# Attention and two feed-forward layers on one core: new fixed costs for VectorE in the scheduler's table, and a new set of priorities

## The chip, the cores and the metric

The kernel runs on 1 core of one Trainium2 chip. TensorE (PE) does the matmuls, VectorE (DVE), ScalarE (ACT) and GpSimd (POOL) the elementwise work, and SyncE (SP) issues every DMA on one hardware queue. The metric is the device time of one execution in microseconds: the median of several runs.

## The reference

Masked attention over 4 batches, 8 heads, 576 positions and head size 64, followed by two feed-forward layers over the 2304 resulting tokens (model size 512, inner size 2048). The weights and alpha come as float64.

```python
scores = scale * np.matmul(q, k.transpose(0, 1, 3, 2))
mask = block_i >= block_j            # blocks of 64 positions
scores = np.where(mask, scores, -1000000000.0)
scores = scores - np.max(scores, axis=-1, keepdims=True)
attn = np.exp(scores)
attn = attn / (np.sum(attn, axis=-1, keepdims=True) + 1e-09)
x = np.matmul(attn, v)               # then heads side by side: [2304, 512]
h = x @ w_in;  x = (np.maximum(h, 0.0) + alpha * np.minimum(h, 0.0)) @ w_out
h = x @ w_in2; x = (h * (1.0 / (1.0 + np.exp(-1.702 * h)))) @ w_out2
```

## The kernel before

**Attention** runs in 20 passes: for batch 0 four head pairs with the first 320 queries and then the same four with the other 256; for batches 1 to 3 one pass per head pair with both groups of queries. Of a pass, PE transposes q and k (tile `tp`, line 345), ACT and DVE split them into a high and a low part (tiles `k`, `ks`, `qs`; lines 120, 123, 388), and PE makes negated scores (tile `sc`, line 441). DVE masks and takes the minimum of each row (lines 455, 456), ACT takes the exponential with its row sum (tile `e`, line 464), DVE the reciprocal of the sums (tile `stat`, lines 473, 474), POOL the fp16 high part of the normalised weights and DVE its fp16 remainder (tile `hl`, lines 486, 494). A DMA transposes `hl` into `pt` (line 498). PE multiplies `pt` with the values (tile `pv`, line 519), and ACT and DVE add the two halves of `pv` into `x` (lines 531, 532). Transposes `tp` and products `pv` share two PSUM buffers (tag `tv`), so that the next `tp` or `pv` but one waits for line 532 of a `pv`.

**The feed-forward layers** use each matmul three times, with high and low parts in fp32r. While attention still runs, PE does half of the first layer's inner features (8 of 16 blocks `f`) for token blocks of 288: line 207 (tile `h`), the gate on ACT and DVE (lines 215, 216), the split on ACT and POOL (tile `gs`), and the second product (tile `x2`, lines 245 to 247). After attention come the other 8 blocks of the first layer and then the second layer, in token blocks of 384 (lines 207, 218, 219, 653, 663, 666). Each weight block of 128 x 512 float64 words is loaded as integers (tile `rw`), and turned into fp32 by ACT and three DVE instructions (lines 150, 153, 155, 156; tiles `wa`, `sq`), then split (`wh`, `wl`). Matmuls of a small constant tile (`warm`, line 584) fill gaps on PE at the start.

**The order of the instructions** is made by the program itself. The functions put pieces of work on a list, each with a place in time plus a value by kind: `at()` adds `0.1 * ORDER[kind] + SHIFT[kind]`. After everything has been recorded, `arrange()` (line 782 on) plays the work through a model: it keeps for each engine a heap of the instructions that are ready, takes the one with the lowest value as soon as the engine is free, adds the duration that `cost()` (line 758 on) gives, and writes the order that results as fixed dependencies. The engines then run their queues strictly in this order. So the table in `cost()` decides when something is ready in the model, and `SHIFT` which of the ready pieces goes first.

```python
    def at(kind, n, fn):
        plan.append((n, ORDER[kind], len(plan), fn, n + 0.1 * ORDER[kind] + SHIFT.get(kind, 0)))
```

The lines that the change touches are the table `SHIFT` (lines 48 to 55) and one line of `cost()` (line 776), for DVE: reads of PSUM with fewer than three operands, instructions under 8 elements, and `tensor_reduce`.

Of the kernel before, what the change touches and what calls it, by code (L numbers as in the profile page):

```python
# [45 lines left out]
    "split x 2": 8, "load w": 9, "load w 2": 9, "load x": 9, "load k": 9.5, "load q": 9.5, "load v": 9.5, "load alpha": 9.6,  # L46
}
SHIFT = {
    "gate": -44.2, "gate 2": -23, "gemm1": 56.7, "gemm1 2": 12.5, "gemm2": 12.8, "half": 58.9, "half out": -42,
    "high": -6.3, "load alpha": 27.7, "load k": 56.1, "load q": -37.1, "load v": -27.1, "load w": -32.6,  # L50
    "load w 2": -53.5, "load x": -33, "narrow": 56.5, "narrow 2": -25.1, "norm": -46.2, "out": -53.7,
    "prep out": 42.4, "prep t": 41.2, "prep v": 41.6, "pv": -10, "pv out": -41.9, "rest": 40.6, "score": 51.7,
    "setup": -24.2, "soft": 19, "split g": -43.8, "split g 2": 4.8, "split w": 7.8, "split w 2": -28.1,
    "split x": 26.4, "split x 2": 57.1, "warm": 56.9,
}
BIG = 1.0e30

# [655 lines left out]
def free_size(ap):  # L713
    n = 1
    for _, c in list(ap.ap)[1:]:
        n *= c
    return n
# [40 lines left out]
def cost(eng, kind, ins, outs):  # L758

    n = max(free_size(a) for a in ins + outs)  # L760
    psum = any(a.tensor.space == PSUM for a in ins)
    if eng == "PE":
        mv, w = ins[:2]
        cols, load = free_size(outs[0]) * (2 if mv.dtype == F32 else 1), free_size(w)
        rows = list(w.ap)[0][1]
        each = 13.3 if mv.dtype == F32R else 2.7
        return cols / 2.4 + each, load / 1.2 + 13.3 if BYTES[w.dtype] == 4 else load / 4.8, cols * rows / 128, mode(w)
    if eng == "Activation":
        return (50 if psum else 93) + n / 1.2 + (187 if len(outs) > 1 else 0),
    full = sum(free_size(a) == n for a in ins)  # L770
    if eng == "Pool":
        return (35 + n / 1.2 if not ins else 244 + n / 1.2 if full < 2 else 148 + 2.1 * n),
    if not ins:
        return (40 if outs[0].tensor.space == PSUM else 7) + n / 1.92,
    if psum and len(ins) < 3 or n < 8 or kind == "InstTensorReduce":
        return 65 + n / 0.96,
    if full < 2:
        return 64 + n / 1.92,
    return (129 if len(ins) > 2 else 68) + n / 0.96,
# [174 lines left out]
```

## Time and profile before

| | |
|---|---|
| median of 3 runs | 1086.78 us (1085.62 to 1089.73) |
| profiled execution | 1087.33 us, its span 1085.5 us |
| PE busy | 1021.4 us (94% of the span), 6454 matmuls |
| DVE busy | 604.3 us (56%), 1029 instructions |
| ACT, POOL busy | 494.7 us (46%), 462.4 us (43%) |
| DMA | 120.28 MB, 111 GB/s |
| mean granted TensorE clock | 0.982 of 2.4 GHz |

The shares are means over stages with different limits. The page's slices cut the span into 40 equal parts of 27.1 us; attention ends near 423 us, and from about 484 us on PE is nearly always busy. In the rows below, "idle before" is the time in which an engine stood still just ahead of an instruction, with the instruction whose end let it go on.

### The profile page before, as it was taken

To read this page: it belongs to the slowest core of one execution; us is meant where nothing else is said; L and a number is where in the kernel's file an instruction comes from. 1 tells how busy PE (TensorE), PEld (TensorE's weight loads), DVE (VectorE), ACT (ScalarE), POOL (GpSimd) and SP (SyncE) were. 2 spreads that over 40 slices of the span, in tenths; PEclk is the share of its full clock that TensorE was granted. 3 is DMA by queue.
4 is the path that set the end of the run, shared out by engine and by line. 5 is a ranking of instruction groups with operands and counts; after the bars stand their busy time and mean duration, and the time that the engine had idled before them with its cause. 6 is when DMAs were issued, how large, how long until landed. Compare 5 with 4: busy or idle time off the path is not lost. (4 is left out here: it accounts for less than half of the span.)

```text
span 1085.5 us, 17180 instructions
## 1 busy us (share of the span) xinstructions
PE 1021.4 (94%) x6454; PEld 934.3 (86%) x6454; DVE 604.3 (56%) x1029; ACT 494.7 (46%) x1164; POOL 462.4 (43%) x494
## 2 busy tenths in 40 slices
PE   7776978999999999999999999999999999999998
PEld 4554867989898899999999999899999999999997
DVE  7888998788888885778883236831111121211110
ACT  5664765666566564565543235433223232322322
POOL 4565864656666574644432233422222222222221
PEclk8888999999999999999999999999999999999999
DMA  7897989788989765544643225401000010000000
GB/s 190 189 209 156 209 188 187 138 176 155 175 154 175 147 124 140 168 141 157 202 144 126 81 65 183 146 8 59 1 30 30 1 59 1 30 30 1 30 1 30
DMA packets 257284, 120.28 MB, mean 111 GB/s; under 512 B 213936, under 2 KB 250800, under 8 KB 257200
## 3 DMA queue, kind: packets, MB, share of 16 engines
q1 hardware_dynamic: 257200, 119.18, 46.1%
q8 instruction: 51, 0.84, 0.3%
q14 instruction: 33, 0.27, 0.1%
HBM read 68.82 MB, written 18.87 MB: 81 GB/s over the span
## 5 line engine op out<-in xcount | busy, mean ns | idle before, releaser
L123 POOL TENSOR_TENSOR gs<-g,gs 128x384 fp32r<-128x384 f32 (+1 forms) x208 | 212.8, 1024 | 452.4 <-ACT gs L120 431.8
L207 PE MATMUL h<-xh,wh 128*128 128x384 f32 (+1 forms) x832 | 272.2, 327 | 6.8 <-ACT xo L251 3.7
L207 PE MATMUL h<-xh,wl 128*128 128x384 f32 (+1 forms) x832 | 270.2, 325 | 0.0
L219 DVE TENSOR_TENSOR g<-g,h 128x384 f32<-128x384 f32 x96 | 53.1, 553 | 291.6 <-ACT g L218 291.6
L653 PE MATMUL acc<-wh,gs 128*128 128x512 f32 x576 | 194.9, 392 | 1.5 <-DVE o L663 1.5
L207 PE MATMUL h<-xl,wh 128*128 128x384 f32 x576 | 193.1, 335 | 0.0
L207 PEld LDWEIGHTS h<-xh,wh 128*128 128x128 f32 x832 | 156.3, 188 | 15.3 <-ACT xo L251 5.2
L207 PEld LDWEIGHTS h<-xh,wl 128*128 128x128 f32 x832 | 156.4, 188 | 0.1
L120 ACT ACTIVATE gs<-g 128x384 fp32r<-128x384 f32 (+1 forms) x208 | 103.3, 498 | 106.7 <-DVE g L219 60.9
L218 ACT ACTIVATE g<-h 128x384 f32<-128x384 f32 x96 | 47.0, 490 | 191.6 <-PE h L207 191.6
L486 POOL TENSOR_SCALAR hl<-e,stat 64x64 f16<-64x64 f32 (+4 forms) x160 | 107.7, 688 | 57.1 <-DVE stat L474 28.0
L653 PEld LDWEIGHTS acc<-wh,gs 128*128 128x128 f32 x576 | 108.1, 188 | 22.4 <-DVE o L663 1.3
L494 DVE SCALAR_TENSOR_TENSOR hl<-e,stat,hl 64x64 f16<-64x64 f32 (+4 forms) x160 | 122.7, 800 | 5.7 <-POOL hl L486 4.7
L653 PE MATMUL acc<-wl,gs 128*128 128x512 f32 x288 | 113.7, 395 | 0.0
L207 PEld LDWEIGHTS h<-xl,wh 128*128 128x128 f32 x576 | 108.1, 188 | 4.1
L519 PE MATMUL pv<-pt,vp 128*128 128x256 f16 (+2 forms) x960 | 88.1, 248 | 14.6 <-DMA pt<-hl 10.5
L464 ACT ACTIVATE e<-sc,stat 64x64 f32<-64x64 f32 (+4 forms) x160 | 82.8, 520 | 34.0 <-DVE hl L494 19.2
L653 PE MATMUL acc<-gs,wh 128*128 128x384 f32 x384 | 98.1, 335 | 0.2 <-DVE o L663 0.2
L216 DVE SCALAR_TENSOR_TENSOR g<-g,nalph,h 128x288 f32<-128x288 f32 (+1 forms) x112 | 61.6, 551 | 58.4 <-ACT g L215 57.4
L519 PEld LDWEIGHTS <-vp 128*128 128x128 bf16 x960 | 64.6, 102 | 27.6 <-DMA pt<-hl 14.9
L123 POOL TENSOR_TENSOR wl<-sq,wh 128x512 fp32r<-128x512 f32 x40 | 59.5, 1488 | 61.7 <-ACT wh L120 61.6
L245 PE MATMUL x<-gs,wh 128*128 128x288 f32 x256 | 75.7, 302 | 2.9 <-ACT wh L120 2.4
(65 smaller groups left out, 1708.4 us busy)
## 6 DMA issues: line engine op xcount, KB each, us to landing
rw<-in_moe_w_in_dram SPq DMA_DIRECT2D x32, 512.0 KB, 4.2
rw<-in_moe_w_out_dram SPq DMA_DIRECT2D x32, 512.0 KB, 3.8
nat_q<-in_q_dram SPq DMA_DIRECT2D x24, 288.0 KB, 4.1
nat_k<-in_k_dram SPq DMA_DIRECT2D x16, 288.0 KB, 3.6
nat_v<-in_v_dram SPq DMA_DIRECT2D x16, 288.0 KB, 4.5
xa<-xo SPq DMA_DIRECT2D x32, 144.0 KB, 2.5
o<-xa SPq DMA_DIRECT2D x24, 192.0 KB, 2.5
xl<-xs SPq DMA_DIRECT2D x6, 768.0 KB, 4.9
```

Of the source, the lines that this page charges most:

```text
L120: act.activation(out=dst, in_=src, func=ACTF.Copy, scale=scale_)
L123: eng.tensor_tensor(out=dst, in0=src, in1=hi.bitcast(F32), op=ALU.subtract)
L207: pe.matmul(ps, st_[:, sl], mv[:, c], start=z == 0, stop=z == 3 * KD - 1)
L216: dve.scalar_tensor_tensor(out=g, in0=g, scalar=nalph[:, f:f + 1], in1=ps, op0=ALU.mult, op1=ALU.add)
L218: act.activation(out=g, in_=ps, func=ACTF.Sigmoid, scale=1.702)
L219: dve.tensor_tensor(out=g, in0=g, in1=ps, op=ALU.mult)
L245: pe.matmul(ps, oh[:, sl], gh, start=f == 0, stop=False)
L464: act.activation(out=eo, in_=v[:, h] if len(heads) > 1 else v, func=ACTF.Exp, scale=-1.0, bias=stat[0:m, 0, a:a + 1], accum_out=stat[0:m, ...
L486: pool.tensor_scalar(out=o, in0=e, scalar1=r, scalar2=1.0, op0=ALU.mult, op1=ALU.mult)
L494: dve.scalar_tensor_tensor(out=hl_part(j, 1, m, nk, h), in0=es[h][0:m, off:off + nk], scalar=stat[0:m, 2, 2 * a + h:2 * a + h + 1], in1=hl ...
L519: pe.matmul(o, l, r, start=z == 0, stop=z == len(ops) - 1)
L653: pe.matmul(ps, a, b_, start=f == f0 and z == 0, stop=f == NF - 1 and z == 2)
```

## The change

One line of the DVE price in `cost()` goes from 65 ns to 155 ns of fixed time for instructions of 8 or more elements, and all 33 values of `SHIFT` are replaced. No instruction is added, removed or changed; the queues hold the same instructions in another order.

```diff
 SHIFT = {
-    "gate": -44.2, "gate 2": -23, "gemm1": 56.7, "gemm1 2": 12.5, "gemm2": 12.8, "half": 58.9, "half out": -42,
...
+    "gate": -35, "gate 2": -14, "gemm1": 42.8, "gemm1 2": 46.1, "gemm2": 47.4, "half": 42.2, "half out": -36.5,
...
     if psum and len(ins) < 3 or n < 8 or kind == "InstTensorReduce":
-        return 65 + n / 0.96,
+        return (65 if n < 8 else 155) + n / 0.96,
```

SP, the first instructions of its queue, before: loads of `q`, `v`, the first weight block, `k` and alpha.

```order
L322 DMA nat_q<-in_q_dram 128x7x64
L325 DMA nat_v<-in_v_dram 128x7x64
L137 DMA rw<-in_moe_w_in_dram 128x4x128
L325 DMA nat_k<-in_k_dram 128x9x64
L574 DMA nalph<-in_moe_alpha_dram 128x16x1
L322 DMA nat_q<-in_q_dram 128x7x64
```

And now:

```order
L325 DMA nat_k<-in_k_dram 128x9x64
L322 DMA nat_q<-in_q_dram 128x7x64
L137 DMA rw<-in_moe_w_in_dram 128x4x128
L325 DMA nat_v<-in_v_dram 128x7x64
L574 DMA nalph<-in_moe_alpha_dram 128x16x1
L322 DMA nat_q<-in_q_dram 128x7x64
```

The load of `k` has gone from the fourth place to the first; the second load of `q` (the same rows, for the other half of the partitions) is still the sixth.

DVE in batch 1, about 189 us into the trace of before: `x` from the product `pv_2124` of one pass, and the six remainders `hl00`, `hl01` of the next pass, before:

```order
L473 TENSOR_SCALAR stat0_100<-stat0_100 128x6
L474 RECIPROCAL stat0_100<-stat0_100 128x6
L532 SCALAR_TENSOR_TENSOR x_1765<-pv_2124,x_1765 64x256
L494 SCALAR_TENSOR_TENSOR hl00_96<-e_2077,stat0_100,hl00_96 64x64
L455 MEMSET sc_2240 64x64
L494 SCALAR_TENSOR_TENSOR hl00_96<-e_2077,stat0_100,hl00_96 128x192
L216 SCALAR_TENSOR_TENSOR g_2222<-g_2222,nalph_78,h_2191 128x288
L494 SCALAR_TENSOR_TENSOR hl00_96<-e_2156,stat0_100,hl00_96 128x320
L494 SCALAR_TENSOR_TENSOR hl01_97<-e_2078,stat0_100,hl01_97 64x64
L216 SCALAR_TENSOR_TENSOR g_2311<-g_2311,nalph_78,h_2253 128x288
L494 SCALAR_TENSOR_TENSOR hl01_97<-e_2078,stat0_100,hl01_97 128x192
```

And now:

```order
L494 SCALAR_TENSOR_TENSOR hl00_96<-e_2077,stat0_100,hl00_96 128x192
L494 SCALAR_TENSOR_TENSOR hl00_96<-e_2156,stat0_100,hl00_96 128x320
L388 SCALAR_TENSOR_TENSOR qs_2162<-tp_2110,qs_2162 128x512
L494 SCALAR_TENSOR_TENSOR hl01_97<-e_2078,stat0_100,hl01_97 64x64
L494 SCALAR_TENSOR_TENSOR hl01_97<-e_2078,stat0_100,hl01_97 128x192
L494 SCALAR_TENSOR_TENSOR hl01_97<-e_2157,stat0_100,hl01_97 128x320
L216 SCALAR_TENSOR_TENSOR g_2349<-g_2349,nalph_78,h_2290 128x288
L456 TENSOR_REDUCE stat1_101<-sc_2240 128x1
L455 MEMSET sc_2241 64x64
L532 SCALAR_TENSOR_TENSOR x_1765<-pv_2124,x_1765 64x256
```

Line 532 of `pv_2124` was the 300th instruction of the queue, ahead of all six remainders, and is now the 312th, behind all of them; the first of the remainders is the 301st in both.

PE in batch 2, about 320 us into the trace of before: the product `pv_3920` of the second head of a pass, behind second products `x2` of the first layer, before:

```order
L245 MATMUL x2_4096<-gs_79,wh1_1265 128x288
L246 MATMUL x2_4096<-gs_79,wh1_1265 128x288
L247 MATMUL x2_4096<-gs_79,wl1_1266 128x288
L245 MATMUL x2_4096<-gs_79,wh1_1315 128x288
L519 LDWEIGHTS vp1_95
L519 MATMUL pv_3920<-pt_3858,vp1_95 128x256
```

And now, behind the last matmuls of `pv_3863`, the product of the first head of the same pass:

```order
L519 MATMUL pv_3863<-pt_3822,vp1_95 128x256
L519 LDWEIGHTS vp1_95
L519 MATMUL pv_3863<-pt_3822,vp1_95 128x256
L519 LDWEIGHTS vp1_95
L519 MATMUL pv_3920<-pt_3858,vp1_95 128x256
```

Between the two products stood 37 matmuls of other work, and now none; ahead of `pv_3920` stand 52 matmuls fewer than before (2041 against 2093).

## Rows read from the trace of the kernel before

**Rows 1.** The page's slices: busy tenths of PE and DVE and the granted clock of PE in 40 equal parts of the span.

```profile
PE   7776978999999999999999999999999999999998
DVE  7888998788888885778883236831111121211110
...
PEclk8888999999999999999999999999999999999999
```

**Rows 2.** Stretches of the span: from and to, length, then busy us (and instructions) of PE, PE's weight loads, DVE, ACT and POOL, the granted clock, DMA's busy share and GB/s.

```profile
0.00:30.00 30.00, 20.64 (x105) 13.04 (x106) 23.27 (x43) 15.58 (x37) 13.76 (x27) 0.89 0.79 189
30.00:130.00 100.00, 77.59 (x551) 58.90 (x549) 85.55 (x160) 59.88 (x154) 64.20 (x66) 0.88 0.87 187
130.00:240.00 110.00, 95.01 (x774) 85.96 (x773) 93.17 (x182) 67.72 (x194) 63.44 (x76) 0.97 0.90 178
240.00:410.00 170.00, 162.05 (x1395) 152.23 (x1393) 144.32 (x284) 108.27 (x317) 109.64 (x137) 1.00 0.81 153
410.00:484.00 74.00, 71.47 (x519) 69.16 (x518) 51.97 (x71) 38.93 (x85) 35.41 (x31) 1.00 0.53 156
484.00:1086.00 602.00, 594.66 (x3121) 554.97 (x3119) 205.97 (x293) 204.28 (x380) 175.99 (x160) 1.00 0.20 65
```

**Rows 3.** What PE waited for between 30 and 423 us: total us, times, longest.

```profile
PE pv L519 <- DMA pt<-hl: 10.5, 9, 4.0
...
PE x L245 <- ACT wh L120: 2.4, 1, 2.4
...
PE x L247 <- POOL wl L123: 1.6, 1, 1.6
PE pv L519 <- DVE x L532: 1.6, 2, 1.0
...
PE tp L345 <- DVE x L532: 0.8, 2, 0.5
```

**Rows 4.** What DVE waited for longest, in three stretches: 0 to 423 us, 0 to 240 us and 240 to 410 us, in this order. In each of the three it is the first row.

```profile
DVE x L532 <- ACT x L531: 26.7, 31, 5.3
...
DVE x L532 <- ACT x L531: 12.8, 13, 3.5
...
DVE x L532 <- ACT x L531: 7.6, 16, 1.5
```

**Rows 5.** Groups of DVE instructions by line and shape: count, busy us and mean ns of one.

```profile
L219 DVE TENSOR_TENSOR g<-g,h 128x384 f32<-128x384 f32 x96 | 53.1, 553 | 291.6 <-ACT g L218 291.6
...
L456 DVE TENSOR_REDUCE stat<-sc 128x1 f32<-128x576 f32 x32 | 23.9, 748 | 0.4
...
L532 DVE SCALAR_TENSOR_TENSOR x<-pv,x 64x320 f32<-64x320 f32 x32 | 15.8, 493 | 9.4 <-ACT x L531 8.8
```

**Rows 6.** PE's instructions in order of time at the start: start, us, what, and idle before.

```profile
8.66 1.08 PE L345 MATMUL tp<-ident,nat_k 128*128 128x128 f32 x4 [2.62 <-DMA nat_k<-in_k_dram]
9.54 2.51 PE L584 MATMUL warm<-mk_l 128*128 128x384 bf16 x8
11.89 0.49 PE L345 MATMUL tp<-ident,nat_q 128*128 128x128 f32 x3
...
21.74 0.72 PE L345 MATMUL tp<-ident,nat_q 128*128 128x128 f32 x3 [2.50 <-DMA nat_q<-in_q_dram]
```

**Rows 7.** SP's issues in order of time at the start: start, us that the issue took, what.

```profile
0.74 0.45 SPq L322 DMA_DIRECT2D nat_q<-in_q_dram  x1
...
2.44 0.52 SPq L325 DMA_DIRECT2D nat_k<-in_k_dram  x1
...
16.46 0.37 SPq L137 DMA_DIRECT2D rw<-in_moe_w_in_dram  x1
16.92 0.46 SPq L322 DMA_DIRECT2D nat_q<-in_q_dram  x1
```

**Rows 8.** DVE's instructions in order of time, around its two longest waits for `pv` ahead of 410 us.

```profile
103.09 0.69 DVE L156 SCALAR_TENSOR_TENSOR sq<-rw,wa 128x512 int32<-128x512 int32 x1
107.24 0.43 DVE L532 SCALAR_TENSOR_TENSOR x<-pv,x 64x256 f32<-64x256 f32 x1 [3.45 <-ACT x L531]
...
189.06 0.19 DVE L474 RECIPROCAL stat<-stat 128x6 f32<-128x6 f32 x1
192.53 0.42 DVE L532 SCALAR_TENSOR_TENSOR x<-pv,x 64x256 f32<-64x256 f32 x1 [3.29 <-ACT x L531]
192.88 0.27 DVE L494 SCALAR_TENSOR_TENSOR hl<-e,stat,hl 64x64 f16<-64x64 f32 x1
```

**Rows 9.** The same of the last two products of attention.

```profile
417.30 0.42 DVE L532 SCALAR_TENSOR_TENSOR x<-pv,x 64x256 f32<-64x256 f32 x1 [5.30 <-ACT x L531]
...
422.30 0.43 DVE L532 SCALAR_TENSOR_TENSOR x<-pv,x 64x256 f32<-64x256 f32 x1 [0.91 <-ACT x L531]
```

**Rows 10.** PE's instructions in order of time, from `pv_3863` to `pv_3920`.

```profile
315.32 0.93 PE L519 MATMUL pv<-pt,vp 128*128 128x256 f16 x15
...
319.79 0.29 PE L245 MATMUL x<-gs,wh 128*128 128x288 f32 x1
319.92 0.29 PE L246 MATMUL x<-gs,wh 128*128 128x288 f32 x1
...
320.71 1.08 PE L519 MATMUL pv<-pt,vp 128*128 128x256 f16 x12
```

**Rows 11.** The transposes `pt` between 100 and 423 us, from issue to landing.

```profile
DMA to landing us min/median/max: 3.6/4.7/8.3
```

More of the change, by code (lines that the diff above doesn't have):

```diff
@@ L48 @@
 SHIFT = {
-    "gate": -44.2, "gate 2": -23, "gemm1": 56.7, "gemm1 2": 12.5, "gemm2": 12.8, "half": 58.9, "half out": -42,
[L50 to L54, printed above, removed]
+    "gate": -35, "gate 2": -14, "gemm1": 42.8, "gemm1 2": 46.1, "gemm2": 47.4, "half": 42.2, "half out": -36.5,
+    "high": -9.5, "load alpha": 47, "load k": -55.2, "load q": -48.8, "load v": 11, "load w": -23.2,
+    "load w 2": 28.4, "load x": 8.4, "narrow": 25.9, "narrow 2": -9.6, "norm": -60, "out": -9.6,
+    "prep out": -12.5, "prep t": -30.5, "prep v": 31.5, "pv": 24, "pv out": 13.2, "rest": 10.5, "score": -22.6,
+    "setup": 24.1, "soft": 4, "split g": 7.6, "split g 2": -15.6, "split w": 15.3, "split w 2": 52.5,
+    "split x": -41.1, "split x 2": 19.5, "warm": 60,
 }
```

## Prediction

> **What bounds the kernel now.** I read the page's slices first [rows 1]: PE shows 9 tenths in nearly every slice from the tenth on, but 6 to 9 in the nine before, and in the first four its granted clock is 0.8 of full speed, that is a mix of the levels of 1.2 and 2.4 GHz. Then the stretches [rows 2], from which PE's idle time is worked out as length less busy time: 9.4 us in 0 to 30, 22.4 in 30 to 130, 15.0 in 130 to 240, 7.9 in 240 to 410, 2.5 in 410 to 484 and 7.3 in the 602 us after that. From 484 us on the kernel is as long as its matmuls; an order cannot shorten them, so whatever the change gives must come from the 57 us of idle time ahead of that, of which 22.4 + 15.0 + 7.9 = 45.3 us lie where attention runs. There DVE is busy 86%, 85% and 85% of the three stretches, ACT and POOL 58 to 64%: DVE is the engine nearest to its limit beside PE.
>
> What PE names in that time [rows 3] are mostly products `pv` that wait for a transposed `pt` to land (10.5 us in 9 times), then weights for the second products (2.4 and 1.6). `pt` takes 3.6 to 8.3 us, with a median of 4.7, from issue to landing [rows 11], and is issued when the last remainder of its head is made by DVE. So I follow the chain back to DVE and read what DVE waits for [rows 4]: line 532, the addition of the second half of a `pv`, waits 26.7 us for ACT's copy of the first half, 12.8 of it before 240 us and 7.6 from 240 to 410. The two longest before 410 us show how [rows 8]: at 189.25 DVE is done with the reciprocals, and the next thing in its queue is line 532 of `pv_2124`, whose product PE has not made yet; DVE stands 3.29 us, and behind line 532 stand the remainders for the next `pt`. At 107.24 the wait is 3.45.
>
> **The table.** The instructions whose price changes take 553, 748 and 493 ns by the trace [rows 5]. By the old formula (65 + n/0.96) they were priced at 465, 665 and 398, and by the new one (155 + n/0.96) at 555, 755 and 488. The new prices fit within 7 ns, the old ones were 83 to 95 too low. Some 260 such instructions stand ahead of 423 us (96 minima, 48 of `k` and `ks`, 52 `qs`, 64 of `x`, counted in the order), so the old model thought DVE 260 x 0.09 = 23.4 us less loaded than it is. That is by itself no gain: the durations on the chip stay. It says that a DVE which the old model saw arrive at line 532 later or earlier was mistimed, and I take from it only that the new order can be nearer to what the engines do. What the order gives I price from the rows.
>
> **The start, 0 to 30 us.** `k` goes to the front of SP's queue [rows 7]. Before, it was issued at 2.44, and PE's transposes began at 8.66 after a wait of 2.62 [rows 6], 6.22 us behind the issue. The second load of `q` in pass 2 shows the shorter delay, 21.74 - 16.92 = 4.82 us. `k` issued at 0.74 with that delay gives 5.56. But of the 18 warming matmuls ahead of `tp`, eight now stand behind it, together 16 instead of 8 between `tp` of `k` and `tp` of `q`; eight took 2.51. So `tp` of `q` comes at 5.56 + (11.89 - 8.66) + 2.51 = 11.3 instead of 11.89, -0.6; with the longer delay at 12.7, +0.8. In pass 2 the load of `q` now stands ahead of the weight load that took SP from 16.46 to 16.92 [rows 7], and PE waits there 2.50 [rows 6]: -0.4. Together **-1.0**, from -2.6 (the whole first wait) to +0.8.
>
> The Trainium skill, "DMA: Bandwidth & Descriptors", section "Queues, rings and completion order", says that each DMA engine consumes the descriptors of a ring in their order. The second load of `q` is still sixth with the same bytes ahead of it, so by this rule its landing doesn't move, this term would be about 0 and the sum 1082.3. The rows can't tell it apart, as PE came to `tp` of `q` with no wait of its own.
>
> **DVE's waits, 30 to 240 us.** Of 61 instructions of line 532 ahead of 410 us, 55 stand further back in DVE's queue, on average behind 2.5 us of DVE work that was behind them before (their new positions by the order, durations by the trace). `pv_2124` is one: six remainders and six other instructions have gone ahead of it, and its 3.29 us would be filled. Others stay: line 532 of the product at 107.24 is only 0.6 us further back against its `pv`, so most of its 3.45 remains. Of the 12.8 us some 9 are lifted. What reaches the end is less: PE's idle time there has other causes too, and DVE lifted from one wait reaches the next cause, ACT's exponentials or the next `sc`. I take half, **-4.5**, between 0 and -9.
>
> **240 to 410 us.** 7.6 us of such waits [rows 4], in 16 pieces of 1.5 or less, which a displacement by 2.5 us covers. PE's idle time of 7.9 is the ceiling. Half again, -3.8, less what I can't place: **-3.5**, between 0 and -7.6.
>
> **New waits on PE.** The products are drawn forward: before, 37 matmuls of other work stood between `pv_3863` and `pv_3920`, from 316.25 (the end of the first group in [rows 10]) to 320.71, 4.46 us in which the second `pt` could land; now none. Ahead of `pv_3920` stand 52 matmuls fewer. A matmul there takes 0.13 us (two begin at 319.79 and 319.92), so PE comes 52 x 0.133 = 6.9 us earlier if nothing stops it, while the remainders that feed its `pt` stand only 0.4 us earlier on DVE. PE will then wait for `pt` where it waited hardly at all; `pt` takes its 4.7 us regardless. And since `tp` and `pv` share two buffers, a later line 532 keeps them longer: 1.6 and 0.8 us before [rows 3]. Work that is not done while PE waits is not lost: the 37 matmuls come later, and fill gaps that would exist there, but PE has only 7.9 us of idle time to fill in this stretch. The price is between 0 (all of it filled later) and +7 (one full wait of 52 matmuls not given back); the waits before, 10.5 us over 9 times, average 1.2, and three of that size is the nearest row: **+3.5**.
>
> **Edits at nothing.** The last of the first eight output weight blocks is narrowed 6 us of DVE work later. PE waited 2.4 and 1.6 for weights there [rows 3]; now scores of the next pass stand ahead of the matmul that needs them, and cover it: 0, or +3 without that cover. Line 532 of the last two products, 5.30 and 0.91 us of wait [rows 9], keeps its place: 0. From 484 us on the order of PE moves by 2 us at most, and its 7.3 us of idle time belong to the second layer's start: 0, within 2. The granted clock of 0.88 from 30 to 130 [rows 2] follows PE's pauses in that stretch; fewer pauses could lift it and more could lower it, 1 us either way.
>
> **Sum.** -1.0 - 4.5 - 3.5 + 3.5 = -5.5. The profiled execution took 1087.33 (span 1085.5 and 1.83 around it) and would take 1081.8; the median of the runs lies 0.55 below the profiled one, so the forecast of the median is 1086.8 - 5.5 = **1081.3**. 0.5% of the time is 5.4 us, about what a measurement can tell from no change, and the forecast stands on that edge.
>
> **Rivals.**
> *PE stands at the products instead of DVE at line 532.* DVE keeps its pace, as its shares of 85% are work and its waits move to the exponentials; PE arrives earlier at `pv` and waits the whole 6.9 us once more than is given back. Then -1.0 + 7 = +6, 1092.8. It decides when less than about 1 us of the two DVE terms reaches the end. For it speaks that `pt`'s 10.5 us are PE's largest wait already; against it, that these matmuls have a full queue of other products behind them whose operands are there. Chance 0.16, and 0.12 of that slower by over 0.5%.
> *The waits change their name only.* DVE no longer stands at line 532, but at ACT or POOL, or PE at DMAs; ACT and POOL are idle 36 to 42% of the stretches, which speaks against them as bounds, DMA's share of 0.81 to 0.90 [rows 2] speaks for the transfers as one. Gains and new waits within 2: 1085 to 1088. Chance 0.20.
> *All is lifted and nothing comes back.* -1 - 9 - 7 = -17, 1069.8. DVE's 85% in 30 to 410 (323 of 380 us) would have to become 89%. For it: the table now fits the chip, and the model can interleave without surprise. Against: PE's idle time in those stretches has at least four causes. Chance 0.12.
> *The forecast*, 0.52, with a range of its own from 1077 to 1086; 0.30 of it faster by over 0.5%, 0.22 within.
>
> Faster 0.12 + 0.30 = 0.42; slower 0.12; within 0.5% 0.46. The range of eight in ten leaves out half of the third rival and some of the first: 1073 to 1092.5.
>
> **What would show it.** The start: `tp` of `k` near 5.6 us and `tp` of `q` near 11.3. DVE's waits: line 532 for ACT, 26.7 us in all before, at some 12 or less, with DVE's busy share in 30 to 240 at 87% or more. New waits: PE's `pv` for `pt` above 10.5, and `tp` or `pv` for line 532 above 1.6 and 0.8. Busy times from 484 us to the end unchanged within 2 us, only earlier. It is wrong if line 532 still waits its 20 us, if the idle time of PE in 240 to 410 grows above 7.9, or if a difference comes from behind 484 us.

## The result and the profile after

The changed kernel takes 1098.43 us (median of 4 runs, 1097.2 to 1099.98) against 1086.2 us for the kernel before (4 runs, 1083.25 to 1089.73): a ratio of 1.0112, 95% interval 1.0079 to 1.0145. It is slower by 12.2 us, outside the predicted range. The profiled execution took 1097.2 us with a span of 1095.4 us, 9.9 us more than the span before; the mean granted clock fell from 0.982 to 0.974.

The slices of the page, as in [rows 1]: busy tenths of PE and DVE, and PE's granted clock.

```profile
PE   7777969989999899999999999999999999999998
...
DVE  7889888879888775788884235941111121211110
...
PEclk8788989989999899999999999999999999999999
```

In the ninth slice (219 to 246 us) and again in the fourteenth (356 to 383 us) PE and its clock now both show an 8, where [rows 1] has a 9 in all four digits. The stretches, with the columns of [rows 2]:

```profile
0.00:30.00 30.00, 20.67 (x107) 13.10 (x108) 23.65 (x44) 15.01 (x36) 14.51 (x27) 0.89 0.78 184
30.00:130.00 100.00, 79.26 (x550) 60.77 (x548) 85.52 (x158) 60.14 (x157) 61.25 (x65) 0.86 0.87 191
130.00:240.00 110.00, 92.36 (x740) 84.07 (x739) 95.24 (x180) 66.09 (x187) 64.40 (x78) 0.93 0.87 176
240.00:410.00 170.00, 158.50 (x1338) 149.47 (x1336) 141.96 (x274) 107.00 (x308) 99.44 (x127) 0.97 0.75 148
410.00:484.00 74.00, 71.01 (x548) 68.70 (x547) 53.15 (x76) 40.13 (x90) 38.85 (x37) 1.00 0.50 139
484.00:1096.00 612.00, 603.92 (x3181) 564.98 (x3179) 207.71 (x303) 210.89 (x390) 182.78 (x162) 1.00 0.21 67
```

PE's idle time by stretch (length less busy) was 9.4, 22.4, 15.0, 7.9, 2.5 and 7.3 us, and is 9.3, 20.7, 17.6, 11.5, 3.0 and 8.1. Over the whole span PE idles 69.7 us instead of 64.1 and is busy 1025.7 instead of 1021.4 with the same 6454 matmuls. So of the 9.9 us, 5.6 are waits, and 4.3 are longer busy time of the same matmuls, which I put down to the granted clock: 0.93 and 0.97 in 130 to 240 and 240 to 410 us, where [rows 2] has 0.97 and 1.00.

What DVE waited for longest from 0 to 433 us, as in the first of [rows 4] (attention ends some 10 us later now):

```profile
DVE g L216 <- ACT g L215: 11.6, 14, 2.9
DVE sc L455 <- PE sc L441: 10.2, 12, 2.7
DVE x L532 <- ACT x L531: 7.8, 6, 4.7
DVE hl L494 <- POOL hl L486: 6.9, 16, 1.0
DVE stat L473 <- ACT e L464: 6.4, 7, 2.3
```

And the same rows of the kernel before, in so far as [rows 4] doesn't show them:

```profile
DVE g L216 <- ACT g L215: 10.3, 15, 3.1
DVE hl L494 <- POOL hl L486: 4.7, 12, 0.8
...
DVE sc L455 <- PE sc L441: 3.3, 10, 0.5
...
DVE stat L473 <- ACT e L464: 1.8, 6, 0.7
```

Line 532's wait fell from 26.7 to 7.8 us, as foreseen. But DVE's idle time from 30 to 410 us is 14.5 + 14.8 + 28.0 = 57.3 us, and was 14.4 + 16.8 + 25.7 = 57.0 by [rows 2]. The time has moved to other rows: 6.9 us more for PE's scores (line 455), 4.6 more for ACT's exponentials (line 473), 2.2 more for POOL.

What PE waited for from 30 to 433 us, as in [rows 3]:

```profile
PE pv L519 <- DMA pt<-hl: 12.1, 7, 4.4
PE sc L441 <- ACT e L464: 10.7, 13, 2.4
PE x L247 <- POOL wl L123: 6.3, 2, 3.9
PE x L245 <- DVE g L216: 3.8, 1, 3.8
...
PE tp L345 <- DVE x L532: 2.2, 4, 0.9
```

`pv` for `pt` grew by 1.6 us only, line 532 by 0.2 (with 0.4 for `pv`, not shown). The new names are weights for line 247 (1.6 before) and one wait of 3.8 us for line 216.

Where the loss arises is not read from such sums, since a wait can be made good later. I therefore compared two profiles by progress: each matmul is counted by its columns (and a small fixed time, warming ones left out), and the lag at a time t of the kernel before is how much later the other kernel had done the same amount. In us, for the kernels of this study that matter:

```
                 at 160    210    240    300    350    370    510 us
after               4.6   -0.4    4.8    5.6    4.6   10.3    9.9
pool_run_gate       3.6   -0.3    5.1    5.9    4.6    6.3    4.8
vp_behind           4.4    1.3    8.2    9.2   13.8   18.9   21.1
mid_after          -1.5   -4.7   -0.4   -0.1   -0.4   -1.3   -2.2
tail_after          0.4   -2.2    1.3    2.2    0.9    5.8    7.7
end_after          -1.4   -4.6   -4.5   -5.0   -1.0    3.8    4.2
start_after         4.5    2.1    3.7    3.1    2.5    2.4    2.4
```

In this execution the changed kernel is level at 210 us, loses 5.2 us between 210 and 240 (place A) and 5.7 between 350 and 370 (place B), and nothing after that. Each row is a single execution: those of after, mid_after, tail_after and end_after were the fastest of their kernel, that of vp_behind (1109.91 us) the slowest.

**Place A.** PE's instructions in order of time (start, us, what, idle before):

```profile
230.62 0.77 PE L519 MATMUL pv<-pt,vp 128*128 128x128 f16 x6
...
233.74 1.08 PE L441 MATMUL sc<-ks,qs 128*128 128x448 f32 x4 [2.35 <-ACT e L464]
...
236.92 0.37 PE L519 MATMUL pv<-pt,vp 128*128 128x256 f16 x1 [1.67 <-DMA pt<-hl]
```

These are two waits, 4.0 us together, the first for ACT's exponentials (which hold the buffer of `sc`), the second for `pt`. Six matmuls that stood between these scores and this product before (the last of `h_2920` and `h_2943` of the first layer) need an `x` that line 532 of `pv_2614` completes, and that instruction now runs at 235.44, 4.1 us later than before (231.34). That they are the cause is a guess at this point; the run both tests it.

**Place B.** All engines, in order of time:

```profile
357.36 0.80 POOL L123 TENSOR_TENSOR gs<-g,gs 128x288 fp32r<-128x288 f32 x1
357.42 5.33 DVE L494 SCALAR_TENSOR_TENSOR hl<-e,stat,hl 128x320 f16<-128x320 f32 x1 [0.35 <-POOL hl L486]
358.12 1.28 POOL L396 TENSOR_TENSOR nat_v<-nat_v,vp 128x576 f32<-128x576 f32 x1
359.36 3.04 POOL L123 TENSOR_TENSOR xlb<-x,xh 128x288 fp32r<-128x288 f32 x4
362.68 0.50 DVE L216 SCALAR_TENSOR_TENSOR g<-g,nalph,h 128x288 f32<-128x288 f32 x1
363.24 0.61 PE L245 MATMUL x<-gs,wh 128*128 128x288 f32 x1 [3.78 <-DVE g L216]
```

One remainder of 128 x 320, which usually takes 0.53 us, takes 5.33: it begins 60 ns behind the first of six POOL instructions without a gap and ends 0.35 us after the last of them. The gate of line 216 stands behind it on DVE, and PE stands 3.78 us for that gate. The trace books the 5.33 us as busy time of DVE, so no row of DVE's waits names them. In the kernel before, the same remainder (the 136th of the 160) had one POOL instruction beside it, `nat_v`, with a gap ahead of that:

```profile
358.95 1.59 DVE L494 SCALAR_TENSOR_TENSOR hl<-e,stat,hl 128x320 f16<-128x320 f32 x1
```

The granted clock makes the wait dearer. PE's busy time, instructions, clock, DMA share and GB/s in steps of 4 us, at place A and at place B:

```profile
234.00:238.00 4.00, 2.33 (x13) 0.67 1.05 218
238.00:242.00 4.00, 4.00 (x26) 0.50 0.39 92
...
354.00:358.00 4.00, 4.00 (x37) 1.00 0.38 36
358.00:362.00 4.00, 1.45 (x10) 0.96 0.33 70
362.00:366.00 4.00, 2.76 (x11) 0.50 0.53 98
366.00:370.00 4.00, 4.00 (x32) 0.69 0.11 35
370.00:374.00 4.00, 4.00 (x46) 1.00 1.12 218
```

After the wait PE runs at 1.2 GHz and does 11 and 32 matmuls where its full 4 us hold 37 to 46. Of the 5.7 us of lag 3.8 are the wait; the other 1.9 I put down to the clock. At place A the clock is 0.67 and 0.50 in 234 to 242 us (the first two rows).

### The profile page after: what moved, and what is told of

It is laid out like the page before. It is cut to its first block, busy times and chain, and to the rows that moved or that the text cites. A ratio compares the mean times of both kernels' runs of the same rounds, so it can differ in the third digit from the quotient of the medians.

```text
span 1095.4 us, 17169 instructions
## 1 busy us (share of the span) xinstructions
PE 1025.7 (94%) x6454; PEld 941.1 (86%) x6454; DVE 607.2 (55%) x1029; ACT 499.3 (46%) x1164; POOL 461.2 (42%) x494
## 4 chain that ended last, share of the span: by engine, by line
PE 71%; DMA 9%; DVE 8%; ACT 4%; issue 4%; POOL 4%; SPq 1%; ACTq 0%; DVEq 0%; POOLq 0%
PE h L207 30%; PE acc L653 26%; PE pv L519 4%; PE sc L441 3%; DMA pt<-hl 3%; PE x L245 2%; PE x L246 2%; PE x L247 2%; DVE hl L494 2%; POOL hl L486 2%; PE tp L345 2%; DMA nat_k<-in_k_dram 1%; DVE stat L456 1%; DMA rw<-in_moe_w_out_dram 1%; ACT e L464 1%
## 5 line engine op out<-in xcount | busy, mean ns | idle before, releaser
L123 POOL TENSOR_TENSOR gs<-g,gs 128x384 fp32r<-128x384 f32 (+1 forms) x208 | 215.5, 1040 | 459.2 <-ACT gs L120 430.4
L494 DVE SCALAR_TENSOR_TENSOR hl<-e,stat,hl 64x64 f16<-64x64 f32 (+4 forms) x160 | 125.8, 821 | 7.5 <-POOL hl L486 6.9
L519 PE MATMUL pv<-pt,vp 128*128 128x256 f16 (+2 forms) x960 | 93.6, 248 | 15.4 <-DMA pt<-hl 12.1
L247 PE MATMUL x<-gs,wl 128*128 128x288 f32 x256 | 76.3, 302 | 6.3 <-POOL wl L123 6.3
```

What stands on the lines that cost most here:

```text
L123: eng.tensor_tensor(out=dst, in0=src, in1=hi.bitcast(F32), op=ALU.subtract)
L247: pe.matmul(ps, ol[:, sl], gh, start=False, stop=f == NA - 1)
L494: dve.scalar_tensor_tensor(out=hl_part(j, 1, m, nk, h), in0=es[h][0:m, off:off + nk], scalar=stat[0:m, 2, 2 * a + h:2 * a + h + 1], in1=hl ...
L519: pe.matmul(o, l, r, start=z == 0, stop=z == len(ops) - 1)
```

## The experiments

The theory after these readings was: the loss is made at places A and B, each a queue order in which one engine stands behind something it does not need. The rivals: the table's new price (or the new priorities) is bad throughout, or the start or the later weights cost the time. Each ratio below is to the kernel before as it was measured alongside (7 to 19 executions, medians 1084.81 to 1087.06 us).

**Each half of the change alone.**

```diff
 oldshift_newtable: SHIFT as in the kernel before, the new line of cost()
 newshift_oldtable: the new SHIFT, and
-        return (65 if n < 8 else 155) + n / 0.96,
+        return 65 + n / 0.96,
```

> Half of the change: the table with 155 ns of fixed time, and the old priorities. Theory one (places in the order, not the table as such, decide): another order with other places, within 10 us of the kernel before either way, 1080 to 1097. If the better table is worth what I forecast, it alone gives 2 to 6 us, 1080 to 1084. If the new priorities are needed to go with it, it is slower than the kernel before by over 5 us.

> The other half: the new priorities, and the table with 65 ns. If the new priorities by themselves are what costs, the time is near 1098. If they were chosen for the new table only, it is slower than 1098. Theory one says that each order has its own few long waits on PE, and expects 1085 to 1105 with stalls at other places than 231 and 359 us.

Measured: 1101.58 us, ratio 1.0149 (1.0123 to 1.0175), for the table alone, and 1095.78, 1.0111 (1.0069 to 1.0152), for the priorities alone. Each half is slower than the kernel before, and together they are no slower than one alone. That the new prices are nearer to the trace ([rows 5]; in the changed kernel 554 ns for the first of them again) made none of these orders faster. The first time lies outside the 1080 to 1097 expected of it. By the same count of matmuls neither kernel loses anything at place B; the table alone loses some 7 us from 130 to 160, 5 at place A and 5 from 370 to 430, the priorities alone some 8 from 130 to 160. That agrees with other orders having other places, and names no cause for them.

**Place B: four instructions of POOL.** `behind` takes the instructions of a queue that write the first tile from the second, and puts them behind the last that writes the third from the fourth.

```diff
 pool_run:
+    behind("Pool", ("xlb_4745", "x_2933"), ("gs_79", "g_4626"))
 pool_run_gate: that, and the gate ahead of the remainder on DVE
+    behind("DVE", ("hl01_97", "e_4398"), ("g_4575", "h_4512"))
```

> The POOL half of pool_run_gate alone: the four subtractions xlb_4745 behind the splits of g_4575 and g_4626, DVE's order as in the changed kernel. If the run of six POOL instructions is what holds DVE, the remainder of e_4398 takes under 2.3 us instead of 5.33 already here, PE's wait at x2_4613 falls from 3.78 to some 1.5, and the time is 1093 to 1095, nearly all of pool_run_gate's gain. If the place of line 216 behind the remainders is what counts, the wait stays above 3 us and the time at 1097 to 1099.

> The changed kernel with two moves: on POOL the four subtractions xlb_4745 stand behind the two splits gs of g_4575 and g_4626 instead of ahead of them, and on DVE line 494 of e_4398 stands behind line 216 of g_4575. Theory one (two places cost the time: at 359 us PE stands 3.78 us at the second product x2_4613 and then runs some 5 us at half clock, since DVE's remainder of e_4398 took 5.33 us beside six POOL instructions without a gap): the 5.33 us fall to about 2, the wait at x2_4613 to under 1.5 us, the clock of 360 to 370 us stays at 1.00, and the time falls by 4 to 6.5 us to some 1092 to 1094. Theory two (the new order is tighter everywhere, and a wait removed in one place comes back in the next): the wait goes, but the time falls by less than 2 us.

Measured: pool_run 1094.92 us, 1.0093 (1.0058 to 1.0128); pool_run_gate 1093.83, 1.0094 (1.0062 to 1.0126). From the profile of pool_run, in order of time, DVE's remainder and PE's wait:

```profile
355.70 2.34 DVE L494 SCALAR_TENSOR_TENSOR hl<-e,stat,hl 128x320 f16<-128x320 f32 x1 [0.35 <-POOL hl L486]
...
358.51 0.40 PE L245 MATMUL x<-gs,wh 128*128 128x288 f32 x1 [0.79 <-DVE g L216]
```

With two POOL instructions beside it (`gs` and `nat_v`, 2.1 us) instead of six, 5.33 became 2.34, and PE's wait 0.79 instead of 3.78. That shows what held this instruction. The clock also stays at 1.00 from 350 to 370 us, and the lag there rises by 2.1 us instead of 5.7, which bears out that the rest of the loss at B came with the clock. The time fell by 3.5 us in the medians (3.0 against the kernel before, 9.2 behind it instead of 12.2) and by 3.6 in the profiled executions (1093.59 against 1097.2); the intervals of the two ratios overlap, so that the whole kernel gained is likely and not shown. A faster kernel than the one before is not among these.

**Place A: two attempts.** vp_behind moves one POOL instruction, `vp0_94` of line 396, from ahead of the high part `hl10_98` to behind `hl11_99`, so that `pt` may be issued earlier. both is pool_run_gate and vp_behind together with five more moves on SP, DVE, ACT and PE around 231 us, among them line 532 of `pv_2614` and the six matmuls behind it.

```diff
 vp_behind:
+    p = orders["Pool"].index(find("Pool", "hl10_98", "e_2523")[0])
+    i = orders["Pool"].pop(p - 1)
+    orders["Pool"].insert(orders["Pool"].index(find("Pool", "hl11_99", "e_2592")[0]) + 1, i)
 both: the lines above, and
+    behind("DVE", ("x_1765", "pv_2614"), ("hl11_99", "e_2524"))
+    behind("Activation", ("ks_2668", "tp_2627"), ("e_2657", "sc_2605"))
...
```

> The changed kernel with one move: on POOL the subtraction vp0_94 (line 396) at 226.8 us stands behind the four high parts hl10 and hl11 of the pass instead of ahead of them, as before the change. Theory one (the second place: at 231.4 us PE stands 2.35 us at the scores sc_2750 and 1.67 at pv_2709, and runs at half clock for a while): the high parts come 1.27 us earlier, so both waits shrink by about that, and the time falls by 2 to 5 us. Theory two (it comes back in the next place): less than 1.5 us. A third (line 532 of pv_2614, which stands 4.1 us later than before the change and feeds the first layer's input, is what leaves PE without other work there): the waits shrink by 1.3 each at most and one of over 1 us stays.

> pool_run_gate, and the place at 231 us mended on all the engines that are in it: vp0_94 behind the high parts on POOL, the load of nat_v that waits for it behind the two pt on SP (in vp_behind it stood 3.03 us in front of pt_2680), line 532 of pv_2614 and the high part xh made from it earlier on DVE and ACT, ACT's exponentials of sc_2605 ahead of the copies of ks, and six matmuls of h_2920 and h_2943 ahead of pv_2709 on PE. If these two places are the 11 us: PE's waits of 2.35 and 1.67 shrink to about 1.2 and 0.5, the clock of 230 to 245 us stays at 1.00, and the time is 1088 to 1091, 3 to 5 us below pool_run_gate. If a wait removed comes back elsewhere: within 2 us of pool_run_gate.

Measured: vp_behind 1102.9 us, 1.0151 (1.0122 to 1.0181), no better than the changed kernel; both 1099.34, 1.0121 (1.0091 to 1.0151), no gain. SP's queue of vp_behind tells why the first failed (start, us that the issue took):

```profile
230.43 0.45 SPq L322 DMA_DIRECT2D nat_q<-in_q_dram  x1
233.91 0.38 SPq L325 DMA_DIRECT2D nat_v<-in_v_dram  x1
```

The load of `nat_v`, which stands ahead of the transposes on SP, needs the buffer that the moved instruction reads; it waited 3.03 us, and `pt` behind it was issued at 234.41 instead of 231.06. PE's two waits stayed at 2.35 and 1.80. In both they were 1.75 and 1.81, the second now at another score, since moving ACT's copies behind the exponentials had made DVE's `ks` late. Line 532 of `pv_2614` ran at 231.90 there and the six matmuls from 234.70 to 236.5, and yet the lag rose by 5.7 us from 210 to 240. So the late `x` alone is not what costs place A; its cause stays open. Several queues meet there, and freeing one showed the next.

In their profiles vp_behind and both also lost 4.6 and 3.8 us between 300 and 350 us, which the changed kernel does not. At 315.35 in vp_behind (313.40 in both):

```profile
315.35 5.24 DVE L494 SCALAR_TENSOR_TENSOR hl<-e,stat,hl 128x192 f16<-128x192 f32 x1
```

This remainder of `e_3631` stands next to another gapless run of six POOL instructions. In the changed kernel's profile it took 0.95 us beside the same run, begun 63 ns behind POOL's start; here it was 60 and 58 ns behind. A remainder of this shape usually takes 0.40 us, so the same neighbours cost 0.5 us or 4.8. That executions of one kernel fall on either side would explain why pool_run's four times lie between 1092.97 and 1100.18, and it would fit that these two profiles are the slowest executions of their kernels (1109.91 and 1100.88 us). But only one execution of each is profiled, so this is not shown.

**The wait measured by itself.** Two small kernels, which leave out the whole computation, repeat one group: POOL makes a high part, then 0 to 6 more instructions, and DVE makes the remainder as line 494 does. In port_sweep DVE is first kept busy for a time that grows in 64 groups, so that it asks at other moments.

> A kernel by itself that leaves out the whole computation: POOL makes one product of 128x320 that DVE's line 494 kind of instruction (two operands of 128x320, fp16 out) needs, and then 0, 1, 2, 4 or 6 further instructions that nobody needs (subtractions of 128x288, or products of 128x320), one behind the other. If DVE is held until POOL's run ends, DVE's instruction takes 0.54 us with none and some 0.8 us more for each that follows: 1.1 to 1.3, 2, 3.5 and 5.1 us. If it only waits for the instruction that POOL is in, it takes 0.54 to 1.4 us however many follow.

> A kernel by itself that leaves out the whole computation: POOL makes one product and then six subtractions without a gap; DVE begins with the end of the product, is busy for a time that grows from group to group (a memset in 31 or 32 groups, a maximum over a row in as many), and then comes to its two-operand instruction, at another moment of POOL's instruction each time. If being held for the whole run depends on the moment at which DVE asks: some of the groups take as long as the rest of the run (2 to 5 us) and the others 0.5 to 1.4. If the moment has nothing to do with it: none above 1.4 us, and the cause is in what the real kernel's engines do beside it.

From port, in order of time, DVE's remainder beside six subtractions of POOL and with POOL free (start, us, what, idle before):

```profile
21.14 1.07 DVE L50 SCALAR_TENSOR_TENSOR lo<-e,r,first 128x320 f16<-128x320 f32 x1 [0.75 <-POOL first L44]
...
27.96 0.55 DVE L50 SCALAR_TENSOR_TENSOR lo<-e,r,first 128x320 f16<-128x320 f32 x1 [0.76 <-POOL first L44]
```

It took 0.55 us alone and 1.07 with one, two, four or six subtractions behind: it got in after one POOL instruction. In port_sweep all 64 lay between 0.43 and 1.19 us (shortest, median and longest in ns):

```profile
L59 DVE SCALAR_TENSOR_TENSOR lo<-e,r,first x64: 429/702/1186, 7.0 to 435.7; 128x320 f16<-128x320 f32 x64
```

So the moment of asking, which was the theory, does not decide by itself. What makes the kernel's own instruction wait for a whole run stays open.

**The model told of it.** held_new gives the scheduler the rule that a DVE instruction of this kind waits until POOL is free, and lets it make the whole order anew.

```diff
-        for e in names:
+        for e in ("PE", "Pool", "DVE", "Activation", "SP"):
...
+                if e == "DVE" and ports[waiting[e][0][1]] and free["Pool"] > now:
+                    free[e] = free["Pool"]
+                    break
```

> The changed kernel with one more rule in the model that makes the order: a DVE instruction that shares POOL's way to SBUF starts only when POOL has nothing ready, instead of between two POOL instructions. If POOL's runs are most of what the model gets wrong, DVE's longest instruction ahead of 425 us is under 2.5 us, PE has no wait over 2.5 us between 230 and 430 us, and the time is 1083 to 1092. If other things that the model leaves out weigh as much (landing times of DMAs, the clock), the time lies anywhere between 1085 and 1105.

Measured: 1134.01 us, 1.0447 (1.042 to 1.0474), outside both ranges expected. The rule makes DVE wait for a whole run of POOL, where port shows it getting in after one instruction, and the priorities were not chosen for this model; which of the two spoils it stays open. PE's idle time grew to 25.0 us in 30 to 130 and 13.3 in 410 to 484 (20.7 and 3.0 in the changed kernel).

**The order of before, with a part of the order after.** The model is played with both tables and both sets of priorities, and the queues are put together from the two orders, cut at counts of instructions that the kernel before had begun at a given time (the lines are those of a part in the middle, with the order of after between two cuts).

```diff
+    for e, n in cuts.items():
+        by = (old[e], orders[e])
+        rank = {i.name: r for r, i in enumerate(old[e])}
+        n = [0] + n + [len(old[e])]
+        orders[e] = [i for z, v in enumerate((0, 1, 0)) for i in by[v] if n[z] <= rank[i.name] < n[z + 1]]
 head_after: after's order up to 215 us; tail_after: from 215 us; mid_after: 215 to 300; end_after: from 300
 end_run: end_after and the line of pool_run
 start_after: up to 30; early_after: 30 to 130; weights_after: 130 to 180; late_after: 180 to 215
```

> Both orders in one kernel: everything that the kernel before had begun by 215 us stands in the changed kernel's order, and the rest in the order of before. If the time is lost at places behind 215 us, as the count of finished matmuls says (the changed kernel was 0.4 us ahead at 210 us and 4.8 behind at 240), this is within 3 us of the kernel before, 1083 to 1089. If the new order loses everywhere, or what it loses later was sown earlier (buffers and loads left late), it is slower by 4 us or more.

> The other way round: before's order up to 215 us, and the changed kernel's order from there on. If the places behind 215 us are what costs, 1094 to 1100, the changed kernel's time within 4 us. If they come from the state that the first 215 us leave, it is near 1086 to 1090.

> Before's order, with the changed kernel's order between 215 and 300 us only. If the place at 231 us costs its 5.5 us wherever it stands, 1089 to 1092, and PE shows waits of some 2.3 and 1.7 us near 233 to 238 us and a clock under 1.00 behind them. If that place is only a knot of the two halves' seam, within 2 us of before.

> Before's order up to 300 us and the changed kernel's from there on. It has the run of six POOL instructions at 354 to 359 us. If that run holds DVE's remainder for all of its length here too, DVE has an instruction of over 5 us and the time is 1089 to 1093; if DVE gets in between, as at 311 us of the changed kernel (0.95 us against 5.24 for the same instruction in vp_behind and both), it is 1084 to 1088. Single runs may differ by 5 us.

> end_after (1096.1) with the one move of pool_run: on POOL the four subtractions xlb_4745 behind the splits of g_4575 and g_4626. If the run of six is what holds DVE, DVE's remainder of e_4398 falls from 5.33 to about 2.3 us, PE's wait at x2_4613 from 3.78 to under 1.7, and the time by 3 to 6 us to 1090 to 1093; the rest, to before's 1085, is the seam at 300 us (3.03 us of wait at pv_3690). If the run was only late for another reason, 1095 to 1097.

Measured: head_after 1090.29 us, 1.0055 (1.0032 to 1.0077); tail_after 1097.22, 1.0127 (1.0107 to 1.0147); mid_after 1088.18, 1.0045 (1.0028 to 1.0062); end_after 1096.1, 1.0098 (1.0069 to 1.0128); end_run 1092.95, 1.0066 (1.004 to 1.0093).

Place A comes with mid_after, whose lag rises by 4.3 us from 210 to 240; its median lies 3.4 us above the kernel before. PE's instructions:

```profile
228.82 1.85 PE L441 MATMUL sc<-ks,qs 128*128 128x448 f32 x4 [2.35 <-ACT e L464]
...
232.73 0.37 PE L519 MATMUL pv<-pt,vp 128*128 128x256 f16 x1 [1.20 <-DVE stat L456]
```

Place B comes with tail_after and end_after; the second's lag rises by 4.8 us from 350 to 370. DVE and PE in end_after, and then in end_run:

```profile
351.76 5.33 DVE L494 SCALAR_TENSOR_TENSOR hl<-e,stat,hl 128x320 f16<-128x320 f32 x1 [0.35 <-POOL hl L486]
...
357.58 0.40 PE L245 MATMUL x<-gs,wh 128*128 128x288 f32 x1 [3.78 <-DVE g L216]
```

```profile
356.44 2.34 DVE L494 SCALAR_TENSOR_TENSOR hl<-e,stat,hl 128x320 f16<-128x320 f32 x1 [0.35 <-POOL hl L486]
...
359.26 0.40 PE L245 MATMUL x<-gs,wh 128*128 128x288 f32 x1 [0.78 <-DVE g L216]
```

The same 5.33 and 3.78 behind the old order of everything earlier, and the same 2.34 when four POOL instructions move; end_run's median lies 3.2 us below end_after's. The intervals of the two ratios overlap, and the two profiled executions go the other way (1093.28 against 1090.23, end_after's fastest), so what is settled is the wait, and not what it is worth in the whole time.

Over all profiles of the study the two places keep to the order. From 210 to 240 us the five with the changed order there (after, pool_run, pool_run_gate, mid_after, tail_after) lose 3.5 to 5.4 us, and the seven with the old order 0.1 to 2.4. From 350 to 370 the four with the six POOL instructions together (after, vp_behind, tail_after, end_after) lose 4.8 to 5.7, the four in which pool_run's line parts them 1.5 to 2.1, and those with the old order there 0.2 or less.

The hybrids do not add up, however: head and tail lose 5.5 + 12.4 us by their medians where the whole loses 12.2, and mid and end 3.4 + 11.3 where tail alone loses 12.4. Seams cost something: end_after has a wait of 3.02 us for `pt` at 301 us, just behind its cut, and its median lies above the 1089 to 1093 that I expected with place B in it.

> The changed kernel's order for what had begun by 30 us, before's from there on. PE in the kernels with the new start is some 2.8 us behind at 30 us and level again by 130. If that is given back: PE behind by 2 to 4 us at 30 us, within 1.5 at 130, and the time within 3 us of before. If the start is the new head's 3 us: slower by 2 to 5.

> The changed kernel's order between 130 and 180 us only, where the last output weight blocks are made later and the product x2_1613 waits for POOL's low parts (2.44 and 3.86 us in the changed kernel, 1.62 once before). If these late weights are the head's loss: PE 2 to 4 us behind at 160 us and 2 to 3 behind still at 210, time 1087 to 1089. If before loses as much a little later (its waits at 167 and 189 us): behind at 160, level at 210, time within 2 us of before.

> The changed kernel's order between 30 and 130 us only. The start and the weights alone cost nothing that can be measured, and the new order up to 215 us cost 5.5 us. If this stretch is the part that counts: slower than before by 2 to 5 us. If only the whole head together costs: within 1.5 us.

> The changed kernel's order between 180 and 215 us only. In this stretch three profiles with before's order gained some 2.5 us against the fourth. If this is the part of the head that counts: slower than before by 2 to 4 us. If not: within 1.5 us.

Measured: start_after 1087.96 us, 1.0004 (0.9986 to 1.0022); weights_after 1085.7, 0.9989 (0.9972 to 1.0007); early_after 1095.41, 1.0085 (1.0057 to 1.0113); late_after 1091.94, 1.0067 (1.0044 to 1.009). The start and the weights are not it: neither costs a measurable time. The other two parts lose 9.5 and 6.0 us by their medians, more than expected of either (2 to 5 and 2 to 4) and more than head_after that contains them, so they cannot be read as shares. Which part of the head makes its 5.5 us stays open.

## Why the prediction was wrong

**DVE's waits, 30 to 410 us (-4.5 and -3.5): the step that failed.** The row itself came true: 26.7 us became 7.8, below the 12 that I named. What failed is "I take half". Nothing of it shows beyond that row: DVE's idle time from 30 to 410 us was 57.0 and is 57.3, and its busy share is 86%, 87% and 84% against 86%, 85% and 85%. The working even names where lifted time goes ("ACT's exponentials or the next `sc`"), and these are the rows that grew, by 4.6 and 6.9 us. The zero that I gave as an end of both ranges was the value to take. PE's idle time in 240 to 410 grew to 11.5 us, which I had named as a sign that the forecast is wrong.

**New waits on PE (+3.5): the sign right, the place wrong.** At the products I had priced three waits of 1.2 us. `pv` for `pt` rose from 10.5 to 12.1 and line 532 from 2.4 to 2.6 (both rows), +1.8 together. `pv_3920`, for which I had reckoned 6.9 us, came 1.4 us earlier, in a kernel that was some 5 us behind by then, and did not wait for its `pt`. The price was paid at two other places, A with 5.2 us of lag and B with 5.7, and the two experiments that carry them into the old order show them again (4.3 and 4.8).

**What the working lacked.** First, I moved line 532 back by 2.5 us on average and asked only who stands behind it on DVE, and what keeps a PSUM buffer; I did not ask who reads `x`. The first layer's matmuls do, and at A they came later; the run both shows that this alone does not make the loss there. Second, POOL's queue. I priced no term for it, yet the change put six POOL instructions together behind a high part, and place B is what that does. I had also taken DVE's busy share of 85% for work. Line 494's 160 remainders took 800 ns each on average before and take 821 now, while the quick ones of their five shapes take about 0.27, 0.40, 0.53, 0.68 and 0.81 us, 0.54 on average. So some 41 us of DVE's busy time before and 45 now are remainders that last longer than the quick ones (an estimate from these figures), as those of port do beside POOL. The change added little of it in sum, but one long piece ahead of a gate that PE waits for.

The Trainium skill, "SBUF — State Buffer", section "SBUF: two separate sides", says that a DVE instruction with two operands in SBUF and a GpSimd instruction that reads SBUF exclude each other, and that the one which starts first holds the ports for its whole instruction. That the two exclude each other agrees with 0.55 us alone and 1.07 behind one subtraction in port. By one instruction the wait at B would be 0.8 us, the length of `gs`; the trace has 4.8 (5.33 less 0.53), six instructions. There the measurement decides, and a rule that I could have weighed before would have given a sixth of the price.

**The start (-1.0).** `tp` of `k` began at 4.31 us without a wait (I had 5.6), but `tp` of `q` at 10.07 waited for its load:

```profile
4.31 1.06 PE L345 MATMUL tp<-ident,nat_k 128*128 128x128 f32 x4
...
10.07 0.85 PE L345 MATMUL tp<-ident,nat_q 128*128 128x128 f32 x6 [1.39 <-DMA nat_q<-in_q_dram]
...
18.72 0.66 PE L345 MATMUL tp<-ident,nat_k 128*128 128x128 f32 x2 [4.71 <-DMA nat_k<-in_k_dram]
```

So `tp` of `q` came 1.8 us earlier than before, but pass 2 then stands 4.71 us for its `k`, whose `tp` begins at 18.72 us instead of 17.79. From 20 to 40 us the count of matmuls puts the kernel between 2 us ahead and 3 behind, and by start_after nothing of it is left at the end (1.0004). So the term is 0. The Trainium skill, "DMA: Bandwidth & Descriptors", section "Queues, rings and completion order", says that a DMA engine takes the descriptors of a ring in their order, from which I had that the sixth load would not land earlier. It landed 6.1 us behind its issue at 4.17 before, and 5.8 behind 4.08 now, that is at 10.3 and 9.9 us: by that rule, the trace agrees. That the sum came out at 0 as well is not due to it but to pass 2.

**Edits at nothing.** The late weights: "0, or +3 without that cover". The cover was missing; line 247 waited 2.44 and 3.86 us, 6.3 against 1.6. Yet weights_after shows no cost (0.9989), so zero was right, and not for the reason that I gave. The kernel was 4.6 us behind at 160 and level again at 210; how much of that was made good can't be told, as the profile of the kernel before itself loses 2.4 to 3.2 us from 160 to 210 against five of the six others with its order there (all but early_after). The last two products and the time from 484 us on did cost nothing, PE's idle time there growing by 0.8 us.

**The clock (1 us either way).** PE's busy time grew by 4.3 us, which I put down to it: the waits at A and B, 4.0 and 3.8 us, come with stretches at 1.2 GHz, and without the wait at B (pool_run) the clock there stays at 1.00. This term was too small by a factor of four.

**The rivals.** For DVE the rival "the waits change their name only" described what happened; its 1085 to 1088 lacked A and B. "PE stands at the products" had the side and, at 1092.8, was nearest in time of all, but by a mechanism that the trace does not show. For the rest of the 12.2 us, the head, the evidence is a measurement without a place: 5.5 us in head_after, while the changed kernel's own profile is level with the one of before at 210 us. Single profiles of the same order differ by up to 4.7 us there (head_after, with the changed kernel's order up to 215 us, is 4.2 behind where that kernel is level), so one pair of profiles cannot show a loss of this size, and the cause of the head's loss stays open.

## What to carry to other kernels

A wait on an engine that is not the bottleneck is worth what the bottleneck gets from it: before crediting a lifted wait, name the instruction of PE that starts earlier, and take zero if none can be named. When a scheduler reorders queues, follow every reader of each result that becomes late, on all engines, and look for long runs without a gap on GpSimd beside VectorE instructions that another engine waits for. A busy share can hold waiting: compare single instructions with the usual time of their shape. Price a wait on TensorE of some 4 us with the slower clock behind it, here half as much again at place B, and use several executions where the loss looked for is under half a per cent.

## What the runs showed of the hardware

One VectorE instruction with two SBUF operands, of 0.53 us, took 5.33 us beside six GpSimd instructions without a gap, in four kernels (after, vp_behind, end_after and, as 5.34, tail_after), and 2.34 beside two (pool_run, end_run). Another of the same line took 0.95 us beside such a run in one kernel (after) and 5.24 in two others (vp_behind, both), at starts that differ by 5 ns at most against GpSimd's. In a small kernel, 64 of 64 got in after at most one instruction (0.43 to 1.19 us). The condition is unknown.

After a wait of 3.78 us TensorE's granted clock was 0.50 and 0.69 in two steps of 4 us, and around two waits of 2.35 and 1.67 us it was 0.67 and 0.50; 0.50 is the level of 1.2 GHz. After a wait of 0.79 us at the same instruction (pool_run) it stayed at 1.00.
